# Recurrence and two-layer block on one core: rounding of the weights spread over more of the run, w_out's block sums on VectorE, loads in another order, earlier turns of the activations

## The chip, the cores and the metric

One core of a Trainium2 chip. The metric is device time in microseconds (us) of one launch, from the first to the last instruction. Timed runs of one job share their runs of the kernel before on the same chip, and every ratio below is the mean time of one kernel's fast runs over the mean of the other's fast runs in the same rounds, so it is not quite the ratio of the medians quoted.

Engines: PE is TensorE (PEld its weight loads), DVE is VectorE, ACT is ScalarE, POOL is GpSimd, SP is the queue that issues most DMAs.

## The reference

A gated linear recurrence gives x of 3072 tokens by 384 features. A two-layer block follows:

```python
f = 1.0 / (1.0 + np.exp(-f_logit))               # (4, 8, 768, 48)
for t in range(S):
    state = f[:, :, t, :, None] * state + einsum('bhd,bhe->bhde', k[:, :, t], v[:, :, t])
    y[:, :, t] = einsum('bhd,bhde->bhe', q[:, :, t], state)
x = y.transpose(0, 2, 1, 3).reshape(3072, 384)
h = x @ w_in                                     # 384 x 2048, float64 as given
g = h * erf(softplus(h))
out = g @ w_out                                  # 2048 x 384, float64 as given
```

## The kernel before

The recurrence is worked in 24 chunks of 128 tokens (stages d, t, s, y for each chunk), 12 blocks of two chunks. The hidden layer of a block is four groups, each a tile of 128x1024 (512 features by 256 tokens). From block 1 on the projection multiplies sums of blocks, seven products in place of eight, for which it needs sums of the activations (`sum_h`) and of w_out (`sum_w`). The weights come as raw 64-bit words and are rounded on the chip, one Abs on ACT and six instructions on DVE for each of 16 pieces:

```python
# round_piece(i): 96 steps in all
nc.scalar.activation(out=dst, in_=high.bitcast(FP32), func=AF.Abs);  yield
nc.vector.tensor_scalar(...);          yield      # L313
nc.vector.tensor_scalar(...);          yield      # L317
nc.vector.scalar_tensor_tensor(...);   yield      # L322
nc.vector.tensor_scalar(...);          yield      # L326
nc.vector.scalar_tensor_tensor(...);   yield      # L331
nc.vector.tensor_tensor(...)                      # L336
```

The activation of a group is a generator, moved one instruction by each `act_step`. Its buffer e has two copies (`epool`, bufs=2), so the Exp of a group can start only when the product two groups back has read its own:

```python
exp(e, h)                    # ACT, L157
term(xs[0], ...); term(xs[1], ...)      # ACT Tanh, L160
times(e, xs[0], 0); times(e, xs[1], 1)  # DVE, L165
...                          # three steps of nothing
activation(e, e, Tanh)       # ACT, L559
tensor_tensor(h, h, e, mult) # DVE, L561
```

One loop issues everything, slot by slot. In each slot PE gets one matmul of the hidden layer or projection, and the other engines' instructions are issued beside it; each engine then works through its own queue in order:

```python
for it in range(n_blocks):                # "pass" in this text
    gen, n = slots(it)                    # pass 0: 96 slots (blocks 0 and 1), pass 1: 48, pass 2: 48 + 32
    ...
    for s, _ in enumerate(gen):
        due += (1 if s < 42 else 0.6 if s < 72 else 0.3) if it == 0 else 0.42 if it == 1 else 0.6
        while due >= 1:
            weights_step(); due -= 1      # one rounding step
        ...                               # loads; a stage of the recurrence where its slot has come
        if it == 0 and s == 14:
            prepare(2, 0, CPB)            # block 2's logits: a maximum on DVE, Exp and Ln on ACT
        if it < 2:
            step = it == 1 and s % 6 == 3
        elif it == 2:
            step = s % 5 in (1, 3)
        ...
        if step: act_step()
        ...                               # sum_step(): block sums
```

The stages' PSUM tiles (d, two transposes t, y) share a pool of two buffers, `ps_at`; after a transpose ACT copies q's out (L418) and ACT, later DVE, copies k's (L420, L422).

Of the kernel before, what the change touches and what calls it, by code (L numbers as in the profile page):

```python
# [48 lines left out]
ALU = mybir.AluOpType  # L49
# [25 lines left out]
def kernel(  # L75
# [10 lines left out]
    nc = tc.nc  # L86
# [36 lines left out]
    def heads(src, b, c):  # L123
        return src[b, :, c * P : (c + 1) * P, :].rearrange("h t d -> t h d")
# [95 lines left out]
    def load_f(g):  # L220
        b, c = divmod(g, NCH)
        blk, j = divmod(g, CPB)
        if j == 0:
            lts[blk] = lpool.tile([P, CPB, d_model], FP32, name="lt", tag="lt")
        nc.sync.dma_start(
            out=lts[blk][:, j, :].rearrange("t (h d) -> t h d", d=D), in_=heads(f_logit, b, c)
        )

    def load(g, what="qkv", queue=None):
        b, c = divmod(g, NCH)  # L230
        queue = queue or nc.sync
        for src, t, n in ((q, qns[g % NQ], "q"), (k, kns[g % NQ], "k")):
            if n in what:
                queue.dma_start(out=t[:].rearrange("t (h d) -> t h d", d=D), in_=heads(src, b, c))
        if "v" in what:
            queue.dma_start(
                out=vts[g % NV][:].rearrange("t (h d) -> t h d", d=D), in_=heads(v, b, c)
            )

    def half(c):  # L240
        return slice(C * c, C * (c + 1))
# [34 lines left out]
    def home_free(i):  # L276
        return all(x in rounded for x in range(i) if HOMES[x] == HOMES[i])

    def load_piece(i):

        assert home_free(i)
        n = d_ff // n_pieces
        if i < n_pieces:
            dst = w_in_sb[:, :, bass.ts(i, n)]
        else:
            m = n_ft // n_pieces
            j = i - n_pieces
            dst = w_out_sb[:, bass.ts(j, m), :]
        raw = None if wpe == 1 else raw_home(i).bitcast(U32)
        to = dst if wpe == 1 else raw.rearrange("p (t w) -> p t w", t=dst.shape[1])  # L290
        src = w_in[:, bass.ts(i, n * wpe)] if i < n_pieces else w_out[bass.ts(j, m * P), :]
        nc.sync.dma_start(out=to, in_=src.rearrange("(t p) w -> p t w", p=P))
        raws[i] = (dst, raw)
# [75 lines left out]
    def keep_busy(n):  # L369

        for _ in range(n):
            nc.tensor.matmul(busy[-1], lhsT=tri[:], rhs=tri[:], start=True, stop=True)
# [30 lines left out]
    def stage_t(g):  # L403
        if g - 1 in late:
            late.pop(g - 1)()
        pss = []
        for src in (qd, kds[g % 2]):
            ps = ps_at.tile([P, HP, P], FP32, name="ps_t", tag="at")
            flat = src[:].rearrange("t (a r) d -> t a (r d)", r=2)
            for a in range(HP):  # L410
                nc.tensor.transpose(ps[:, a, :], flat[:, a, :], ident[:])  # L411
            pss.append(ps)
            if 0 < g < FIRST and src is qd:
                keep_busy(3)
        qAs[g] = work.tile([P, 2, HP, P], FP32, name="qA", tag="qA")
        kTs[g] = work1.tile([P, HP, P], FP32, name="kT", tag="kT")
        for r in range(2):
            nc.scalar.copy(out=qAs[g][half(r), r], in_=pss[0][half(r)])  # L418
        if g < 9:
            nc.scalar.copy(out=kTs[g][:], in_=pss[1][:])  # L420
        else:
            nc.vector.tensor_copy(out=kTs[g][:], in_=pss[1][:])  # L422
# [188 lines left out]

    sum_places = places()

    def add(out, x, y, op=ALU.add, engine=nc.vector):
        engine.tensor_tensor(out=out, in0=x, in1=y, op=op)  # L615

    def sum_w(gi):
        w = w_out_sb[:, FG * gi : FG * (gi + 1), :]
        b11, b12 = w[:, 0:2, 0:DH], w[:, 0:2, DH:]
        b21, b22 = w[:, 2:4, 0:DH], w[:, 2:4, DH:]  # L620
        t = w_sums(gi)
        add(t[:, 0], b12, b11, ALU.subtract, nc.gpsimd)
        yield
        add(t[:, 1], b22, t[:, 0], ALU.subtract, nc.gpsimd)
        yield
        add(t[:, 2], b22, b12, ALU.subtract, nc.gpsimd)
        yield
        add(t[:, 3], b21, t[:, 1], ALU.subtract, nc.gpsimd)

    def blocks(h):  # L630
        return h[:, 0:2, 0:P], h[:, 2:4, 0:P], h[:, 0:2, P:], h[:, 2:4, P:]
# [158 lines left out]
    with tc.manual_schedule():  # L790

        for t in svs:
# [2 lines left out]
        load_f(0)  # L795
        load(0, "kv", nc.scalar)
        load(0, "q")
        load_f(1)
        load(1, "qk")
        load_f(2)  # L800
        load_piece(0)
        load(1, "v")
        load(2)
        load_piece(1)
        load_piece(2)
        load_f(3)
        nc.gpsimd.memset(tri[:], 1.0)
# [1 line left out]
            out=tri[:], in_=tri[:], pattern=[[1, P]], compare_op=ALU.is_ge, fill=0.0,  # L809
# [43 lines left out]
        def weights_steps(n):  # L853
            for _ in range(n):
                weights_step()
# [5 lines left out]
        keep_busy(6)  # L861
        prepare(0, 1, 2)
        stage_t(0)
        load(3, "qk")
        load_piece(3)
        stage_d(1)
# [42 lines left out]
        due = 0.0  # L909
        for it in range(n_blocks):  # L910
            gen, n = slots(it)
            if it == 0:
                todo = [(stage_s, 2), (stage_y, 2), (stage_d, 3), (stage_t, 3), (stage_s, 3), (stage_y, 3),
                        (stage_d, 4), (stage_t, 4), (stage_d, 5), (stage_s, 4), (stage_t, 5),
                        (stage_y, 4)] + stages(2)[4:]
                at = [1, 5, 6, 12, 16, 23, 34, 42, 48, 52, 60, 74, 76, 80, 88, 94]
            else:
                todo = stages(it + 2) if it + 2 < n_blocks else []
                at = [n * x // 48 for x in (2, 6, 11, 17, 25, 29, 34, 41)] if it == 1 else [int(3 + (n - 13) / max(1, len(todo)) * i) for i in range(len(todo))]
            if ADJACENT <= it + 2 < n_blocks:  # L920

                at = ([0] if it + 2 == ADJACENT else []) + [2, 26, 42, 54, 76, 90]
                at = at[: len(todo)]
            if it + 3 < n_blocks:
                prepare_at = at[todo.index((stage_d, (it + 3) * CPB))] - 14
            at, todo = deque(at), deque(todo)
            for s, _ in enumerate(gen):
                due += (1 if s < 42 else 0.6 if s < 72 else 0.3) if it == 0 else 0.42 if it == 1 else 0.6
                while due >= 1:
                    weights_step()  # L930
                    due -= 1
                if s % 6 == 3:
                    load_more()
                if at and s == at[0]:
                    at.popleft()
                    f, g = todo.popleft()
                    f(g)
                    if f in (stage_y, stage_y_s):
                        if g + NSV < n_chunks:
                            load_sv(g + NSV)  # L940
                        load_to(g + LOOK)
                        if g == 2:
                            load(5, "v")
                            load_piece(7)
                if it == 0 and s == 14:
                    prepare(2, 0, CPB)
                if it == 0 and s == 9:
                    load_f(6)
                    load_f(7)
                if s == n // 2 and it + 4 < n_blocks:  # L950
                    for j in range(CPB):
                        load_f((it + 4) * CPB + j)
                if it + 3 < n_blocks and s == prepare_at:
                    prepare(it + 3, 0, CPB)
                if it < 2:
                    step = it == 1 and s % 6 == 3
                elif it == 2:
                    step = s % 5 in (1, 3)
                else:
                    step = s % 9 in (2, 6)  # L960
                if step:
                    act_step()
                if it == 2:
                    if s == n - 6:
                        to_sum.extend(sum_h(groups[1, gi]) for gi in range(NS))
                    sum_step()
                elif it > 2:
                    if s == n_o and it < n_blocks - 1:
                        to_sum.extend(sum_h(groups[it - 1, gi]) for gi in range(NS))
                    if it == n_blocks - 1 and s % n_o == 40 and s < 2 * n_o:  # L970
                        blk = n_blocks - 2 + s // n_o
                        to_sum.extend(sum_h(groups[blk, gi]) for gi in range(NS))
                    if s < n_o or s % 3 == 0 or it == n_blocks - 1:
                        sum_step()
                if it == n_blocks - 2 and s in (5, 40):
                    next(check)
            assert not todo
# [214 lines left out]
```

## Time and profile before

628.27 us (median of 3 runs). The slots allow to cut the span where the hidden layer's 192nd and 288th matmul record ends (ends of passes 0 and 1), where the first projection's last matmul (L670) ends (pass 2), and at a short wait of the hidden layer for an output sum near 231 us:

| stretch of before | us | what limits it |
|---|---|---|
| start and pass 0, to 105.8 | 105.8 | DVE, rounding |
| pass 1, to 135.2 | 29.4 | PE, near full |
| pass 2, to 192.7 | 57.4 | PE with holes |
| start of pass 3, to 231.6 | 39.0 | a 5.90 us hole, then PE |
| the rest, to 627.6 | 396.0 | PE, full |

The page's busy digits, the stretches by engine, PE's holes and DVE's stretched instructions are in the prediction below with their reading. A timeline's rows hold start, length, engine and line, operation, names, shapes, count, and in brackets the idle time and its releaser.

```profile
140.52 1.06 ACT L157 ACTIVATE e<-Hg 128x1024 f32<-128x1024 f32 x1 [2.00 <-DVE wT L561]
149.03 1.06 ACT L157 ACTIVATE e<-wT 128x1024 f32<-128x1024 f32 x1 [1.98 <-DVE wT L561]
```

In both rows the bracket says that ACT stands for 2 us until DVE has done a product, L561.

### The profile page before, as it was taken

Reading aid. Unit: us, or ns where it says so; the run is one execution under the profiler, and the core shown is the slowest. Engines: PE = TensorE matmul, PEld = TensorE weight load, DVE = VectorE, ACT = ScalarE, POOL = GpSimd, SP = SyncE. Lnnn points to the kernel's source line nnn. Section 1 sums busy time; section 2 is a strip of 40 time slices with the busy share of each in tenths; the row PEclk is TensorE's granted clock in tenths of the full one; section 3 lists DMA queues with packets and bytes.
Section 4 is the critical chain, followed back from the end, with each engine's and each line's share of the span. In section 5 each row is a group of like instructions: output and inputs, shape, how many; then the busy total and the mean of one; then the engine's idle time right before and its main releaser. Section 6 shows DMA issues by size and latency. Waiting matters only on the chain.

```text
span 627.6 us, 13891 instructions
## 1 busy us (share of the span) xinstructions
PE 589.5 (94%) x5777; PEld 524.7 (84%) x5777; DVE 470.2 (75%) x788; ACT 382.4 (61%) x483; POOL 38.4 (6%) x49
## 2 busy tenths in 40 slices
PE   8788699998976999999999999999999999999995
PEld 7567588887644988988998998998998989989995
DVE  4998998695589778678787876797887694756751
ACT  5725457978864457756675776765775656556200
POOL 1000011010176000000000000000000000000000
PEclk9879799999989899999999999999999999999999
DMA  9997743440321043043052052052030000000000
GB/s 200 247 241 215 216 123 63 88 78 12 63 56 26 1 78 76 1 79 75 4 102 52 2 102 51 3 102 52 3 76 14 2 27 1 19 8 1 25 26 29
DMA packets 155587, 41.35 MB, mean 66 GB/s; under 512 B 147328, under 2 KB 150400, under 8 KB 155520
## 3 DMA queue, kind: packets, MB, share of 16 engines
q1 hardware_dynamic: 153440, 40.02, 29.3%
q8 instruction: 47, 0.77, 0.5%
q10 hardware_dynamic: 2080, 0.39, 0.3%
q14 instruction: 20, 0.16, 0.1%
HBM read 35.59 MB, written 4.72 MB: 64 GB/s over the span
## 4 chain that ended last, share of the span: by engine, by line
PE 72%; DVE 12%; issue 6%; ACT 5%; DMA 2%; SPq 1%; POOL 1%; DVEq 0%; ACTq 0%; POOLq 0%
PE ops L717 31%; PE hps L587 29%; PE y L525 3%; PE ps_t L411 2%; PE ops L670 2%; PE ps_d L380 2%; DVE sv L438 1%; PE sc L460 1%; PE sc L468 1%; DVE sv L439 1%; DVE w_in_sb L322 1%; DMA qn<-in_q_dram 1%; DVE qA L496 1%; DVE w_in_sb L336 1%; ACT L160 1%
## 5 line engine op out<-in xcount | busy, mean ns | idle before, releaser
L587 PE MATMUL hps<-xT,w_in_sb 128*128 128x256 f32 x1152 | 264.7, 386 | 7.8 <-DVE w_in_sb L336 4.4
L587 PEld LDWEIGHTS hps<-xT,w_in_sb 128*128 128x128 f32 x1152 | 218.2, 192 | 41.2 <-DVE w_in_sb L336 3.4
L165 DVE SCALAR_TENSOR_TENSOR e<-x,e 128x1024 f32<-128x1024 f32 x96 | 120.2, 1252 | 13.5 <-ACT x L160 13.2
L160 ACT ACTIVATE x<-Hg,serf_bias 128x1024 f32<-128x1024 f32 x88 | 97.6, 1141 | 0.2
L157 ACT ACTIVATE e<-Hg 128x1024 f32<-128x1024 f32 x44 | 46.6, 1058 | 77.0 <-DVE Hg L561 73.2
L717 PE MATMUL ops<-wT,Hg 128*128 128x192 f32 x352 | 87.6, 331 | 0.0
L717 PE MATMUL ops<-wT,scratch 128*128 128x192 f32 x320 | 76.5, 331 | 5.9 <-DVE scratch L615 5.9
L717 PE MATMUL ops<-w_out_sb,Hg 128*128 128x192 f32 x352 | 72.6, 329 | 0.0
L561 DVE TENSOR_TENSOR Hg<-Hg,e 128x1024 f32<-128x1024 f32 x44 | 54.6, 1240 | 22.5 <-ACT e L559 22.4
L717 PEld LDWEIGHTS ops<-wT,Hg 128*128 128x128 f32 x352 | 62.1, 192 | 2.2
L594 ACT COPY Hg<-hps 128x1024 f32<-128x1024 f32 x44 | 44.4, 1010 | 31.0 <-PE hps L587 30.7
L717 PEld LDWEIGHTS ops<-w_out_sb,Hg 128*128 128x128 f32 x352 | 60.7, 192 | 2.6
L717 PEld LDWEIGHTS ops<-wT,scratch 128*128 128x128 f32 x320 | 57.0, 193 | 6.2 <-issue 6.2
L559 ACT ACTIVATE e<-e 128x1024 f32<-128x1024 f32 x48 | 50.4, 1050 | 6.4 <-DVE e L165 6.3
L496 DVE TENSOR_TENSOR qA<-sc,tri 64x256 f32<-64x256 f32 x68 | 28.7, 422 | 22.3 <-PE sc L468 21.3
L725 DVE TENSOR_TENSOR scratch<-scratch,ops 128x384 f32<-128x384 f32 (+1 forms) x44 | 22.2, 504 | 30.3 <-ACT scratch L733 25.0
L418 ACT COPY qA<-ps_t 64x512 f32<-64x512 f32 x48 | 27.7, 578 | 22.5 <-PE ps_t L411 20.6
L395 DVE TENSOR_TENSOR qd<-qn,dp 128x384 f32<-128x384 f32 x24 | 13.4, 556 | 35.6 <-ACT dp L383 34.4
L717 PE MATMUL ops<-w_out_sb,scratch 128*128 128x192 f32 x160 | 39.5, 328 | 0.0
L525 PEld LDWEIGHTS y<-qA,sv 128*32 128x32 f32 x1536 | 24.6, 113 | 17.2 <-issue 9.2
L525 PE MATMUL y<-qA,sv 128*32 128x64 f32 x1536 | 28.9, 226 | 9.3 <-issue 6.9
L438 DVE TENSOR_TENSOR sv<-sc,sv 48x192 f32<-48x192 f32 x80 | 28.4, 354 | 8.3 <-ACT qA L488 6.9
(109 smaller groups left out, 648.9 us busy)
## 6 DMA issues: line engine op xcount, KB each, us to landing
lt<-in_f_logit_dram SPq DMA_DIRECT2D x24, 192.0 KB, 3.8
qn<-in_q_dram SPq DMA_DIRECT2D x24, 192.0 KB, 3.3
out_dram<-scratch SPq DMA_DIRECT2D x12, 384.0 KB, 2.6
kn<-in_k_dram SPq DMA_DIRECT2D x23, 192.0 KB, 3.5
vt<-in_v_dram SPq DMA_DIRECT2D x23, 192.0 KB, 3.6
sv<-in_v_dram SPq DMA_DIRECT2D x84, 48.0 KB, 2.9
w_out_sb<-in_moe_w_in_dram SPq DMA_DIRECT2D x4, 768.0 KB, 6.3
Hg<-in_moe_w_in_dram SPq DMA_DIRECT2D x4, 768.0 KB, 6.4
```

Of the source, the lines that this page charges most:

```text
L157: nc.scalar.activation(out=dst[:], in_=h, func=AF.Exp)
L160: nc.scalar.activation(out=dst[:], in_=h, func=AF.Tanh, bias=serf_bias[:, i : i + 1], scale=SERF_KAB[i][0])
L165: nc.vector.scalar_tensor_tensor(out=e[:], in0=x[:], scalar=SERF_KAB[i][2], in1=e[:], op0=ALU.add, op1=ALU.mult)
L418: nc.scalar.copy(out=qAs[g][half(r), r], in_=pss[0][half(r)])
L438: nc.vector.tensor_tensor(out=new, in0=add, in1=old, op=ALU.add)
L496: nc.vector.tensor_tensor(out=qA[half(1 - r), r, :, half(c)], in0=sc[half(c), r], in1=tri1[half(c)].unsqueeze(1).broadcast_to((C, HP, C)), ...
L525: nc.tensor.matmul(y[M * i : M * (i + 1), kt, half(c)], lhsT=sv[:, r, c, a, o : o + M], rhs=qA[:, r, a, half(c)], start=(n == 0), stop=Tru ...
L559: nc.scalar.activation(out=e[:], in_=e[:], func=AF.Tanh, scale=SERF_C)
L561: nc.vector.tensor_tensor(out=h, in0=h, in1=e[:], op=ALU.mult)
L587: nc.tensor.matmul(hps[:, j, :], lhsT=w_in_sb[:, kt, ft * P : (ft + 1) * P], rhs=xTs[blk][:, kt, :], start=(kt == 0), stop=(kt == n_k - 1),)
L594: nc.scalar.copy(out=gr["h"], in_=hps[:])
L717: nc.tensor.matmul(place[n], lhsT=x[:, j, :], rhs=y, start=(gi == 0 and j == 0 and n in first), stop=(gi == n_g - 1 and j == 1), skip_grou ...
```

## The change

Its intent: round a piece when it is due and not as soon as possible, so that DVE is free for the recurrence in pass 0; take w_out's sums off GpSimd, whose instructions stretch DVE's; bring w_in's first pieces earlier; start the activations in pass 0 so that they are not late in pass 2.

```diff
-        add(t[:, 0], b12, b11, ALU.subtract, nc.gpsimd)
+        add(t[:, 0], b12, b11, ALU.subtract)            # VectorE; likewise the other three
 ...
         load(0, "q")
+        load_piece(0)
         load_f(1)
-        load(1, "qk")
+        load(1, "qkv")
+        load_piece(1)
         load_f(2)
-        load_piece(0)
-        load(1, "v")
         load(2)
-        load_piece(1)
         load_piece(2)
 ...
         stage_t(0)
+        weights_steps(2)
 ...
-                due += (1 if s < 42 else 0.6 if s < 72 else 0.3) if it == 0 else 0.42 if it == 1 else 0.6
+                due += (1 if s < 18 else 0.46 if s < 66 else 0.3) if it == 0 else 0.45
 ...
-                if it < 2:
-                    step = it == 1 and s % 6 == 3
+                if it == 0:
+                    step = s >= 24 and s % 8 == 5
+                elif it == 1:
+                    step = s % 5 == 3
```

More of the change, by code (lines that the diff above doesn't have):

```diff
@@ L612, with add @@
     sum_places = places()
-    def add(out, x, y, op=ALU.add, engine=nc.vector):
-        engine.tensor_tensor(out=out, in0=x, in1=y, op=op)
+    def add(out, x, y, op=ALU.add):
+        nc.vector.tensor_tensor(out=out, in0=x, in1=y, op=op)
     def sum_w(gi):
@@ L621, in sum_w @@
         t = w_sums(gi)
-        add(t[:, 0], b12, b11, ALU.subtract, nc.gpsimd)
+        add(t[:, 0], b12, b11, ALU.subtract)
         yield
-        add(t[:, 1], b22, t[:, 0], ALU.subtract, nc.gpsimd)
+        add(t[:, 1], b22, t[:, 0], ALU.subtract)
         yield
-        add(t[:, 2], b22, b12, ALU.subtract, nc.gpsimd)
+        add(t[:, 2], b22, b12, ALU.subtract)
         yield
-        add(t[:, 3], b21, t[:, 1], ALU.subtract, nc.gpsimd)
+        add(t[:, 3], b21, t[:, 1], ALU.subtract)
     def blocks(h):
```

## The prediction

> **What bounds the kernel now.** I read first the page's busy shares in 40 slices (15.7 us each), to see whether one limit holds for the whole span.
>
> ```profile
> PE   8788699998976999999999999999999999999995
> DVE  4998998695589778678787876797887694756751
> PEclk9879799999989899999999999999999999999999
> DMA  9997743440321043043052052052030000000000
> ```
>
> TensorE (PE) is full from slice 14 (220 us) to the end. Only the first 210 us have holes, and there VectorE (DVE) stands at 8 or 9 in slices 2 to 6. I then cut the early part at the program's own stages, told from the order of matmuls: to 28.3 us the start; 28.3 to 105.7 pass 0 (the loop's first 96 slots, one logical matmul a slot, recorded as two); to 135.2 pass 1 (48 slots); to 192.5 pass 2 (48 slots of the hidden layer, 32 of the first projection). The busy-time table by stretch, pass 0 split at 54.3 and pass 2 at 164.3 (columns: stretch, length, busy PE, PEld, DVE, ACT, POOL, granted clock, DMA share, GB/s):
>
> ```profile
> 28.28:54.30 26.02, 23.01 (x258) 18.31 (x258) 23.17 (x43) 10.88 (x19) 0.48 (x1) 0.75 0.88 208
> 54.30:105.70 51.40, 44.19 (x478) 36.66 (x478) 48.77 (x78) 25.91 (x42) 5.32 (x8) 0.93 0.61 162
> 105.70:135.20 29.50, 29.09 (x374) 24.41 (x374) 22.07 (x38) 26.84 (x39) 3.15 (x4) 1.00 0.42 73
> 135.20:164.30 29.10, 27.00 (x302) 22.14 (x300) 17.37 (x24) 23.48 (x29) 1.50 (x2) 1.00 0.29 52
> 164.30:192.50 28.20, 24.42 (x136) 15.16 (x137) 23.55 (x24) 18.96 (x24) 18.10 (x14) 0.94 0.24 43
> 192.50:203.00 10.50, 4.60 (x84) 3.77 (x82) 10.30 (x15) 5.63 (x7) 6.30 (x5) 0.95 0.16 39
> ```
>
> Pass 0 has DVE busy 71.9 of 77.4 us: it is DVE's. Passes 1 and 2 have DVE idle for 7 and 12 us. So DVE is overloaded early and idle in the middle. The last row is again DVE's: 10.30 of 10.5. The holes behind this, from PE's timeline (the bracket is the idle time before the row and its releaser):
>
> ```profile
> 28.28 2.05 PE L587 MATMUL hps<-xT,w_in_sb 128*128 128x256 f32 x4 [1.44 <-DVE w_in_sb L336]
> 45.34 1.22 PE L587 MATMUL hps<-xT,w_in_sb 128*128 128x256 f32 x2 [2.99 <-DVE w_in_sb L336]
> 72.22 1.09 PE L411 MATMUL ps_t<-ident,qd 128*128 128x128 f32 x4 [5.62 <-DVE qd L395]
> 178.22 2.05 PE L525 MATMUL y<-qA,sv 128*32 128x64 f32 x64 [3.78 <-issue]
> 203.00 0.98 PE L717 MATMUL ops<-wT,scratch 128*128 128x192 f32 x2 [5.90 <-DVE scratch L615]
> ```
>
> The first two wait for a rounded piece of w_in. The third waits for qd, a small product that stood in DVE's queue behind roundings of pieces not yet needed. The last waits for block sums of the activations while GpSimd (POOL) was computing w_out's block sums. To see what those do to DVE I compared its groups between 172 and 199 us, and after 203 us when POOL is quiet:
>
> ```profile
> L165 DVE SCALAR_TENSOR_TENSOR e<-x,e 128x1024 f32<-128x1024 f32 x6 | 10.4, 1740 | 1.0 <-ACT x L160 1.0
> L615 DVE TENSOR_TENSOR scratch<-Hg 128x256 f32<-128x256 f32 x2 | 2.4, 1220 | 0.0
> ...
> L165 DVE SCALAR_TENSOR_TENSOR e<-x,e 128x1024 f32<-128x1024 f32 x18 | 22.0, 1220 | 2.7 <-ACT x L160 2.6
> L615 DVE TENSOR_TENSOR scratch<-Hg 128x256 f32<-128x256 f32 x9 | 3.8, 419 | 0.0
> ```
>
> Beside POOL's sums an activation product takes 1.74 us in place of 1.22, a block sum 1.22 in place of 0.42.
>
> **What the Trainium skill says.** "SBUF — State Buffer", Who interferes with whom: a DVE instruction with two SBUF inputs contends with a GpSimd instruction that reads SBUF, and one blocks for the whole of the other. The trace agrees: the two-input forms grow by 0.5 to 0.8 us beside POOL's 1 to 2 us sums. "GPSIMD Engine Reference", Elementwise — side-by-side cycle accounting, has GpSimd 1.96 times as slow as DVE on a float32 tensor_tensor; here one w_out sum takes 0.99 to 1.99 us on POOL, and DVE's product of the same 128x384 size (qd) takes 0.556. "TensorE: Matmul & The Clock Gate", Why this matters for your kernels: avoid PE idle gaps over about 3 us, or the clock halves. The trace agrees: the clock is 0.50 from 30 to 38 us; after the 5.90 us gap a projection matmul starts 0.32 us after the one before it until about 208.5, then 0.16. So a closed gap is worth more than its length.
>
> **The change part by part.** One piece of raw words costs DVE two ops of 0.555, one of 0.56 and three of 0.96, so 4.55 us; the 16 pieces take 96 steps, 0.76 us each, and one 0.92 us Abs on ScalarE (ACT) a piece.
>
> (a) Rate. Before, 10 steps precede the loop, and pass 0 takes 42 + 18 + 7 = 67, pass 1 the rest. After, 12 precede it, then 18 + 22 + 9 = 49 in pass 0, 22 in pass 1, some 13 in pass 2 (over by its slot 30, before the projection at 48 needs w_out). Pass 0 loses 18 steps, 13.7 us of DVE; pass 1 gains about 2 us, pass 2 10 us. Due times hold: w_in's piece 4 is needed at slot 36 and ready at 18, piece 7 needed at 66, ready at 57.
>
> (b) Activation. Before, steps ran 0, 8, 32 in passes 0 to 2; after, 9, 10, 32. Ten steps take one group through, five start the next, so this is some 2 groups earlier: each 3.66 us of DVE (three ops of 1.22) and 4.4 us of ACT (1.06 + 2 x 1.15 + 1.05). It moves about 8 us of DVE work ahead of the first block sums. This is not saved work.
>
> (c) w_out's sums. 16 x 0.555 = 8.9 us more on DVE. Adding up the excess of each DVE op over its quiet length from 172 to 199 us gives 9.8 us of slowing, which goes. DVE's total is level or 1 us better, and POOL's 16 sums (23.4 us together in its timeline, ending at 198.9) leave the path.
>
> (d) Loads. Chunk tensors move at about 215 GB/s, pieces at 340 to 390 (from the start cut in 0.75 us slices). w_in's first piece then lands near 7.5 us in place of 12.5, and chunk 1's logits near 8.4, used at 9.03 before: no loss. Chunk 2's logits land near 14.2 against a use at 13.5, about 1 us late. The two early rounding ops fill DVE's idle time there. I expect the first hidden matmul to stay at 28 to 29 us.
>
> Replaying the queues by hand with these durations:
> Pass 0 to slot 24: piece 2 is ready near 42 in place of 45.3, so that 3 us gap closes; DVE stays full, because the first pieces are due as fast as it can make them, and slot 24 comes only 1.5 to 2 us sooner. Slots 24 to 96: PE's own work is 144 x 0.216 + 10.6 us for the attention stages, about 42; before they took 48.2 (57.5 to 105.7). DVE's is 28 steps (21.3), attention (11.4), three activation products (3.7), so 36.4, and fits. The 5.62 us gap and the slow clock after it go. Pass 0 saves 7.7 us.
> Pass 1: PE 28.4, DVE about 26, ACT about 27: length unchanged, 29 us.
> Pass 2: PE's own work is 20.7 + 20.8 + 7.6 = 49 of the 57.3 before. In its first 30 slots DVE is asked for 3.2 us in every 2.15 us of PE and falls 6 to 8 us behind; most uses stand 12 to 17 slots after their issue, which forgives about 8. ACT too is asked for about 35 us in 26, as before. I give back half of the 8 us: 3 to 4 saved.
> Pass 3's start: the 5.90 us gap and about 2.7 us of half clock after it. DVE will still be some 3 to 5 us behind, so I count 4 to 6 of these 8.6.
> Sum: 7.7 + 3.5 + 5 = 16.2, plus about 1 for a 1.07 us wait at 231 us, which has the same backlog behind it: 17. After that PE is full in both kernels and the savings simply shift the end: 628.3 - 17 = 611.
>
> A check from DVE alone: it has worked 163 us when the sum that ends the last gap is done (202.9 us). After: 163 + 8 (activations) + 8.9 - 9.8 = 170, of which 5 before 12.6 us. At 95% busy: 12.6 + 165 / 0.95 = 186, that is 17 us sooner, with the clock's 2.7 on top, if passes 0 to 2 balance nearly perfectly. They won't quite, so this is the good end, 608.
>
> **Rivals.** *DVE becomes the bound of pass 2.* For: it takes rounding, sums and activations together there. Against: it had 12 us idle in it. If the backlog lasts to the first block sums, pass 2 saves nothing and the gap at pass 3's start stays: only pass 0's 8 us are left, 619 to 620.
> *ACT becomes the bound.* Its copies free the PSUM buffers of the hidden layer, and in pass 2 they already lag by up to 8 us (a 0.77 and a 0.42 us wait of PE show it). If its Tanh also waits for a late DVE, PE stalls more: 616 to 618.
> *The start slips.* If the early piece delays chunk 1 and 2 more than I count, 2 to 3 us are lost, cancelling the early gain: 613 to 614.
> *Everything balances*: DVE's figure plus the clock, 605 to 608.
>
> **Range and chances.** 2% is 615.7 us. The central replay and the good end lie below, with the slipping start; the two engine-bound rivals lie above. No part adds work to PE or to the steady passes, so slower is nearly out. Predicted 611, range 602 to 620; faster by over 2% 0.67, within 2% 0.32, slower 0.01.
>
> **What will show it.** POOL at about 15 us busy (38.4 now, less 23.4 for the sums), and the two-input DVE ops at 1.22 and 0.42 throughout. No 5.62 us wait for qd; pass 0 ending near 98. Rounding instructions until about 145 us. The first matmul on block sums waiting under 3 us. It would be wrong if pass 2 takes 57 us again with PE waiting for DVE or ACT (then work was only moved), or if the start passes 30 us.

## The result, and the profile after

633.21 us median (633.04 to 633.91, 4 runs) against 628.72; ratio 1.0075, 95% interval 1.0049 to 1.0102. So the kernel is within 2% and a little slower, where 611 us was forecast and 602 to 620 given as the range. The profiled runs are 631.6 and 627.6 us long. The busy digits of the changed kernel, 40 slices of 15.8 us:

```profile
PE   7977999986898999999999999999999999999895
DVE  4998696899689976787877795897787783746651
POOL 1000001110000000000000000000000000000000
PEclk8877999999799899999999999999999999999999
```

Counted from 1, POOL is empty from slice 10 on, and DVE is lower in slices 5 and 7 and higher in 8, 10 and 11, as the change wants it. But PE has a 6 in slice 10 (142 to 158 us) and the clock a 7 in slice 11, where before stood 8 and 9. The same cuts as before give:

| stretch | before | after | difference | the prediction's |
|---|---|---|---|---|
| start and pass 0 | 105.8 | 104.8 | -1.0 | -7.7 |
| pass 1 | 29.4 | 32.6 | +3.2 | 0 |
| pass 2 | 57.4 | 60.9 | +3.5 | -3.5 |
| start of pass 3 | 39.0 | 35.3 | -3.7 | -6 |
| the rest | 396.0 | 398.0 | +2.0 | 0 |
| sum | 627.6 | 631.6 | +4.0 | -17 |

The first row holds the start too: the first hidden matmul comes at 30.09 us, before at 28.28, so the pass itself gained 2.8.

The engines from slot 24 to the end of pass 0, in pass 1, and in the 48 slots of the hidden layer in pass 2 (columns as in the prediction):

```profile
60.58:104.76 44.18, 43.91 (x414) 36.20 (x414) 33.28 (x55) 31.82 (x46) 3.26 (x6) 0.94 0.59 153
104.76:137.33 32.57, 29.54 (x374) 24.40 (x374) 27.36 (x42) 26.63 (x40) 4.62 (x4) 1.00 0.38 67
137.33:173.50 36.17, 29.23 (x300) 24.13 (x299) 29.87 (x41) 25.29 (x32) 1.50 (x2) 0.86 0.23 41
```

From 60.58 us on in pass 0, DVE works only 33.28 of 44.18 us: it has 11 us to spare where it was the bound. In the hidden part of pass 2 it works 29.87 of 36.17 us, against 17.37 of 29.10 in the prediction's cut of that part before. The spare time was made in one place and the work put down in another. PE's holes:

```profile
57.19 0.43 PE L525 MATMUL y<-qA,sv 128*32 128x64 f32 x4 [3.43 <-POOL qA L491]
60.58 7.70 PE L587 MATMUL hps<-xT,w_in_sb 128*128 128x256 f32 x22 [0.57 <-ACT xT L529]
72.20 0.60 PE L411 MATMUL ps_t<-ident,qd 128*128 128x128 f32 x4
...
159.49 2.05 PE L525 MATMUL y<-qA,sv 128*32 128x64 f32 x64 [6.94 <-issue]
...
206.09 1.01 PE L717 MATMUL ops<-wT,scratch 128*128 128x192 f32 x2 [3.41 <-DVE scratch L615]
```

The 5.62 us wait for qd has gone: the row at 72.20 has no bracket. It starts at the same time as before, 72.22. The holes of 1.44 and 2.99 us for w_in have gone as well. In their place there is a hole of 3.43 us at 57 us with 22 matmuls at 0.35 us each behind it (7.70 us, where the same 22 took 5.02 before), and one of 6.94 us in pass 2, again with half clock behind it (y takes 2.05 us, where the same y took 1.21 before). The hole before the block sums shrank from 5.90 to 3.41.

How the 6.94 us come about is in the timelines of ACT and DVE between 139 and 160 us. ACT first:

```profile
139.47 1.05 ACT L559 ACTIVATE e<-e 128x1024 f32<-128x1024 f32 x1
140.78 0.48 ACT L386 ACTIVATE kd<-ps_d 128x384 f32<-128x384 f32 x1
146.78 1.06 ACT L157 ACTIVATE e<-Hg 128x1024 f32<-128x1024 f32 x1 [5.51 <-DVE Hg L561]
...
157.15 1.06 ACT L157 ACTIVATE e<-wT 128x1024 f32<-128x1024 f32 x1 [3.04 <-DVE wT L561]
158.22 1.17 ACT L418 COPY qA<-ps_t 64x512 f32<-64x512 f32 x2
```

and DVE:

```profile
141.05 0.56 DVE L326 TENSOR_SCALAR Hg<-w_out_sb 128x768 uint32<-128x768 uint32 x1
141.65 0.96 DVE L331 SCALAR_TENSOR_TENSOR Hg<-Hg 128x768 f32<-128x768 uint32 x1
142.52 1.22 DVE L165 SCALAR_TENSOR_TENSOR e<-x,e 128x1024 f32<-128x1024 f32 x1
143.66 0.95 DVE L336 TENSOR_TENSOR w_out_sb<-Hg,w_out_sb 128x768 f32<-128x768 f32 x1
...
145.46 1.22 DVE L561 TENSOR_TENSOR Hg<-Hg,e 128x1024 f32<-128x1024 f32 x1
```

The Tanh that L561 needs was done at 140.5. L561 stood in DVE's queue for 5 us more, behind four rounding instructions (from 140.06), one activation product and qd and kd. Until then ACT could not start the next Exp, because that Exp writes the buffer that L561 reads, and everything behind the Exp in ACT's queue waited too: the Exp at 157.15 held the copies L418 of the ninth chunk's transposed q, which PE had made at 148. y's weight load starts at 159.46, 0.07 us after those copies end (158.22 + 1.17 = 159.39). y takes its PSUM buffer from the same pool of two. In the runs undo_act, late and pace below the same 0.07 us stand between the two, which is why I take the buffer for the link.

That DVE is no longer stretched beside POOL is plain from its groups between 172 and 199 us, the counterpart of the groups in the prediction:

```profile
L165 DVE SCALAR_TENSOR_TENSOR e<-x,e 128x1024 f32<-128x1024 f32 x7 | 8.5, 1219 | 0.0
L615 DVE TENSOR_TENSOR wT<-w_out_sb 128x384 f32<-128x384 f32 x6 | 3.3, 552 | 0.0
L615 DVE TENSOR_TENSOR scratch<-Hg 128x256 f32<-128x256 f32 x1 | 0.4, 418 | 0.0
```

### The profile page after: what moved, and what is told of

Read it like the earlier page. It is cut to its first block, busy times and chain, and to the rows that moved or that the text cites. A ratio compares the mean times of both kernels' runs of the same rounds, so it can differ in the third digit from the quotient of the medians.

```text
span 631.6 us, 13869 instructions
## 1 busy us (share of the span) xinstructions
PE 593.2 (94%) x5777; PEld 526.2 (83%) x5777; DVE 467.7 (74%) x804; ACT 383.9 (61%) x485; POOL 15.4 (2%) x33
## 4 chain that ended last, share of the span: by engine, by line
PE 68%; DVE 16%; ACT 7%; issue 3%; DMA 3%; SPq 2%; POOL 0%; ACTq 0%; DVEq 0%
PE ops L717 29%; PE hps L587 27%; PE ops L670 3%; PE y L525 3%; PE ps_t L411 2%; DVE sv L438 2%; DVE e L165 2%; DVE sv L439 2%; DVE qA L496 1%; ACT x L160 1%; PE ps_d L380 1%; PE sc L460 1%; PE sc L468 1%; DMA sv<-in_v_dram 1%; ACT L160 1%
## 5 line engine op out<-in xcount | busy, mean ns | idle before, releaser
L165 DVE SCALAR_TENSOR_TENSOR e<-x,e 128x1024 f32<-128x1024 f32 x96 | 117.5, 1224 | 15.5 <-ACT x L160 15.2
L561 DVE TENSOR_TENSOR Hg<-Hg,e 128x1024 f32<-128x1024 f32 x44 | 53.7, 1221 | 17.6 <-ACT e L559 17.4
L717 PEld LDWEIGHTS ops<-wT,scratch 128*128 128x128 f32 x320 | 56.6, 193 | 3.7 <-DVE scratch L615 3.7
L559 ACT ACTIVATE e<-e 128x1024 f32<-128x1024 f32 x48 | 50.4, 1051 | 6.6 <-DVE e L165 6.5
L525 PE MATMUL y<-qA,sv 128*32 128x64 f32 x1536 | 31.5, 230 | 17.7 <-issue 10.2
L525 PEld LDWEIGHTS y<-qA,sv 128*32 128x32 f32 x1536 | 25.9, 116 | 26.6 <-issue 18.8
L725 DVE TENSOR_TENSOR scratch<-scratch,ops 128x384 f32<-128x384 f32 (+1 forms) x44 | 22.1, 503 | 32.5 <-ACT scratch L733 27.2
L418 ACT COPY qA<-ps_t 64x512 f32<-64x512 f32 x48 | 27.7, 577 | 7.3 <-PE ps_t L411 7.0
```

Source lines behind the costliest of these rows:

```text
L165: nc.vector.scalar_tensor_tensor(out=e[:], in0=x[:], scalar=SERF_KAB[i][2], in1=e[:], op0=ALU.add, op1=ALU.mult)
L418: nc.scalar.copy(out=qAs[g][half(r), r], in_=pss[0][half(r)])
L525: nc.tensor.matmul(y[M * i : M * (i + 1), kt, half(c)], lhsT=sv[:, r, c, a, o : o + M], rhs=qA[:, r, a, half(c)], start=(n == 0), stop=Tru ...
L559: nc.scalar.activation(out=e[:], in_=e[:], func=AF.Tanh, scale=SERF_C)
L561: nc.vector.tensor_tensor(out=h, in0=h, in1=e[:], op=ALU.mult)
L717: nc.tensor.matmul(place[n], lhsT=x[:, j, :], rhs=y, start=(gi == 0 and j == 0 and n in first), stop=(gi == n_g - 1 and j == 1), skip_grou ...
```

## The experiments

Theory 1: rounding moved into pass 2 makes DVE late there, and the lateness reaches PE through ACT's queue. Theory 2: w_out's sums on DVE are what costs. Theory 3: the start slips and costs it. Each kernel's profile, cut as above. The profile is one run, and differences under 2 us in its passes 0 to 2 are not to be read alone: before and sums_only issue the same instructions through pass 0, and it took 105.8 and 107.3 us; undo_act and late do so too, with 103.0 and 103.9. One reason for this can be seen in the traces: the granted clock is either 1.00 or 0.50, each 0.50 stretch that begins between 10 and 210 us lasts 3.4, 6.8 or 10.2 us, and they don't lie at the same places in two runs of the same instructions (27.8 to 38.1 us in before, 35.5 to 42.4 in sums_only).

| run | median us | ratio to before | pass 0 | pass 1 | pass 2 | pass 3's start | rest |
|---|---|---|---|---|---|---|---|
| before | 628.7 to 629.4 | 1 | 105.8 | 29.4 | 57.4 | 39.0 | 396.0 |
| the change | 633.2 | 1.0075 | 104.8 | 32.6 | 60.9 | 35.3 | 398.0 |
| undo_sums | 639.3 | 1.0153 | 104.6 | 32.6 | 63.2 | 39.0 | 398.3 |
| undo_rate | 634.1 | 1.0069 | 112.9 | 30.7 | 54.0 | 37.0 | 398.5 |
| undo_act | 626.9 | 0.9960 | 103.0 | 30.3 | 60.4 | 34.5 | 396.0 |
| undo_start | 630.6 | 1.0011 | 104.3 | 33.4 | 58.3 | 35.3 | 398.0 |
| late | 627.1 | 0.9966 | 103.9 | 30.3 | 64.3 | 31.4 | 395.6 |
| pace | 619.6 | 0.9862 | 102.7 | 29.4 | 55.0 | 33.1 | 395.6 |
| prep2 | 630.0 | 0.9988 | 101.0 | 32.6 | 60.9 | 36.6 | 398.5 |
| sums_only | 622.4 | 0.9885 | 107.3 | 29.4 | 54.4 | 34.7 | 395.6 |
| act_only | 636.8 | 1.0124 | 109.2 | 30.3 | 59.1 | 39.0 | 397.5 |
| rate_only | 630.7 | 1.0032 | 100.3 | 29.5 | 64.5 | 37.3 | 396.3 |
| pace_prep | 615.5 | 0.9781 | 101.1 | 29.4 | 55.0 | 34.7 | 396.0 |
| pace_prep_start | 614.1 | 0.9761 | 96.1 | 29.5 | 56.6 | 34.4 | 396.0 |

All kernels gave correct results. The changed kernel was timed in its own job only, so a run is set against it through the two ratios to before or, more loosely, by the medians.

**undo_sums**: the change without the sums on VectorE.

```diff
-        add(t[:, 0], b12, b11, ALU.subtract)
+        add(t[:, 0], b12, b11, ALU.subtract, nc.gpsimd)   # and the other three
```

> The changed kernel with w_out's block sums back on GpSimd, all else kept. Theory 1 (rounding moved into the second and third pass makes VectorE late there, and ScalarE stands in its in-order queue behind VectorE): the 6.94 us hole of TensorE near 152 us stays within 1 us, and the hole before the first product on block sums grows from 3.4 back to about 6 us, so 636 us. Theory 2 (the sums on VectorE are what costs): faster, 629 us or less, and the hole near 152 us shrinks.

639.29 us, ratio 1.0153 (1.0135 to 1.0171). The hole near 152 us is again 6.94 us, and the hole before the block sums 6.25 us. Theory 2 falls: the sums on VectorE are a gain of 5 to 6 us in this kernel (4.9 by the two ratios, 6.1 by the medians), more than the 3 us that theory 1 had given them.

**undo_rate**: the change with the old rate.

```diff
-                due += (1 if s < 18 else 0.46 if s < 66 else 0.3) if it == 0 else 0.45
+                due += (1 if s < 42 else 0.6 if s < 72 else 0.3) if it == 0 else 0.42 if it == 1 else 0.6
```

> The changed kernel with the old rounding rate (a step per slot for 42 slots, then 0.6, 0.3, 0.42), all else kept. Theory 1: the 6.94 us hole near 152 us is under 2 us, the 5.6 us wait for qd in the first pass is back, and the third pass (hidden layer and first projection) gets 6 to 9 us shorter; the sum 625 to 629 us. Theory 3 (the start, 1.8 us late, and the earlier activations cost it): the time stays at 632 to 634 us.

634.12 us, ratio 1.0069 (1.0052 to 1.0086): the total missed what theory 1 expected. The places it named behave much as it said: the hole near 152 us is 1.16 us, pass 2 is 6.9 us shorter (60.9 to 54.0), and the wait for qd is back, with 3.09 us and not 5.6. But pass 0 is 8.1 us longer; PE waits there another 2.48 us for ACT's logits. So the new rate is worth 8 us in pass 0 and costs 7 in pass 2 and 2 in pass 1.

**undo_act**: the change with the old activation turns.

```diff
-                if it == 0:
-                    step = s >= 24 and s % 8 == 5
-                elif it == 1:
-                    step = s % 5 == 3
+                if it < 2:
+                    step = it == 1 and s % 6 == 3
```

> The changed kernel with the old activation turns (none in the first pass, 8 steps in the second), all else kept. Theory 1: VectorE has 8 us less to do before the third pass, so the hole near 152 us shrinks to 0 to 3 us, but the activations are then late for the block sums, whose hole grows from 3.4 to 6 us or more; 629 to 633 us. Theory 2: no change of the hole before the sums.

626.85 us, ratio 0.9960 (0.9940 to 0.9980), better than expected, but not for the reason given: the hole near 154 us is still 5.74 us. The gain is 1.8 us in pass 0, 2.3 in pass 1, 2.0 in the rest, and under 1 in pass 2 and at the start of pass 3. And the hole before the sums, for which the early turns were made, became smaller without them: 2.71 us against 3.41. Nothing had been waiting for activations there.

**undo_start**: the change with the old loads and without the two early steps.

```diff
         load(0, "q")
-        load_piece(0)
         load_f(1)
-        load(1, "qkv")
-        load_piece(1)
+        load(1, "qk")
         load_f(2)
+        load_piece(0)
+        load(1, "v")
         load(2)
+        load_piece(1)
 ...
         stage_t(0)
-        weights_steps(2)
```

> The changed kernel with the old order of loads and without the two early rounding steps, all else kept. Theory 3 (the start slips because chunk 1's and chunk 2's logits come behind w_in's pieces): the first hidden matmul comes at 28.3 us in place of 30.1, and the kernel ends 2 us sooner or more, 631 us or less. Theory 1: the start gains 2 us but the hole near 152 us stays above 5 us; 630 to 632 us.

630.55 us (627.77 to 632.76), ratio 1.0011 (0.9974 to 1.0047). The first hidden matmul comes at 28.05 us in place of 30.09; the hole in pass 2 is 4.04 us, where theory 1 had it above 5. Theory 3's figures came true as well (28.3 us, 631 or less). The start does slip by 2 us, but the hole is still there without the slip, so the start is not the whole loss. What it costs, this run doesn't give cleanly: without the two early steps the new rate makes a piece of w_in late, and PE waits for it, at half clock after the wait, as it doesn't in the changed kernel:

```profile
83.13 6.95 PE L587 MATMUL hps<-xT,w_in_sb 128*128 128x256 f32 x18 [3.15 <-DVE w_in_sb L336]
```

**late**: undo_act with the rest of the rounding held back inside pass 2.

```diff
-                due += (1 if s < 18 else 0.46 if s < 66 else 0.3) if it == 0 else 0.45
+                due += (1 if s < 18 else 0.46 if s < 66 else 0.3) if it == 0 else 0 if it == 2 and s < 29 else 0.45
```

> The run undo_act with one edit: the some 13 rounding steps left for the third pass are held back until its slot 29, behind the issue of the eighth chunk's y; they are due by slot 60 or so. Theory 1 (those steps make VectorE late with the activation product, ScalarE's next Exp waits for it and the copies behind the Exp hold TensorE's y): the 5.74 us hole before y near 154 us is under 2 us, and the kernel ends 4 to 6 us before undo_act, at 621 to 623 us. Rival (the hole comes from the number of activations in the pass, not from the rounding): the hole stays over 4 us and the time within 1 us of 627.

627.12 us, ratio 0.9966 (0.9949 to 0.9983). PE's holes in pass 2 of this run:

```profile
151.36 1.22 PE L525 MATMUL y<-qA,sv 128*32 128x64 f32 x64 [1.99 <-issue]
165.33 4.14 PE L670 MATMUL ops<-w_out_sb,wT 128*128 128x384 f32 x12 [1.50 <-ACT Hg L594]
178.19 2.05 PE L525 MATMUL y<-qA,sv 128*32 128x64 f32 x64 [2.69 <-issue]
191.32 7.12 PE L670 MATMUL ops<-w_out_sb,wT 128*128 128x384 f32 x16 [3.73 <-DVE wT L561]
```

The hole before y went from 5.74 to 1.99 us as theory 1 said: the rounding makes it. But the time didn't move. The same DVE work 30 slots later opened 1.50, 2.69 and 3.73 us elsewhere, the last a projection matmul that waits for the product L561 itself. So the fault is not the place of one instruction: at neither of the two places tried did pass 2 have room for the rounding.

**pace**: undo_act with the rest of the rounding done in pass 0's idle time.

```diff
-                due += (1 if s < 18 else 0.46 if s < 66 else 0.3) if it == 0 else 0.45
+                due += (1 if s < 18 else 0.46 if s < 30 else 0.62) if it == 0 else 0.45
```

> The run undo_act with the first pass's rate at 1 a slot up to slot 18, 0.46 up to slot 30, then 0.62, so that no rounding is left for the third pass. VectorE would be busy some 45 of the 45 us from slot 24 on in the first pass. Theory 1: the hole before y near 154 us falls under 2 us; the first pass gets 2 to 4 us longer; 622 to 626 us. If the first pass can't take it, the qd wait is back and the time is 627 to 630 us.

619.57 us (617.64 to 622.11), ratio 0.9862 (0.9833 to 0.9890), 2.4 us below what was expected. Pass 0 is 102.7 us, no longer than without the extra steps (103.0): DVE did have the room. The hole before y is 1.51 us and pass 2 5.4 us shorter than in undo_act, pass 1 0.9; pass 2's 55.0 us are close to the 54.4 of sums_only, which moves no rounding. With late this settles theory 1.

**prep2**: the change with block 2's logits prepared earlier.

```diff
-                if it == 0 and s == 14:
+                if it == 0 and s == 2:
                     prepare(2, 0, CPB)
```

> The changed kernel with the preparation of block 2's logits issued at slot 2 of the first pass in place of slot 14. Theory: the 3.43 us hole before y near 57 us (and the half clock after it, some 2.5 us) comes from ScalarE waiting for VectorE's maximum on these logits with the score copies behind it. Then that hole falls under 1.5 us and the first pass ends 3 to 5 us sooner; the hole near 152 us takes part of it back; 629 to 631 us. Rival (VectorE itself is late there): the hole stays.

629.95 us (625.27 to 631.44), ratio 0.9988 (0.9949 to 1.0028). The hole near 57 us:

```profile
55.85 0.30 PE L525 MATMUL y<-qA,sv 128*32 128x64 f32 x4 [1.59 <-issue]
```

1.59 us in place of 3.43 (just above the 1.5 named), and pass 0 ends 3.8 us sooner. The same kind of link as in pass 2, with another waiter: ACT's Exp of the logits waited for a DVE maximum at the end of a queue of roundings (ACT's wait before it was 3.51 us), and the score copies stood behind it. The hole in pass 2 stayed at 6.94 us, and of 3 us the times show about 3, within a wide spread.

**sums_only**: the kernel before with only the sums on VectorE.

```diff
-        add(t[:, 0], b12, b11, ALU.subtract, nc.gpsimd)
+        add(t[:, 0], b12, b11, ALU.subtract)               # and the other three
```

> The kernel before with only w_out's sums moved to VectorE. Theory: the slowing beside GpSimd (9.8 us of VectorE time) is gone and 8.9 us of sums come in, so VectorE's load is level, but y at 178 us and the block sums are no longer behind stretched instructions: the 3.78 and 5.90 us holes fall to about 1.5 and 3 us, the end 4 to 6 us sooner: 623 to 626 us. Rival (the holes come from lateness alone): within 1 us of the kernel before.

622.42 us, ratio 0.9885 (0.9864 to 0.9907), better than expected. The two holes that stood beside POOL's sums:

```profile
177.44 1.21 PE L525 MATMUL y<-qA,sv 128*32 128x64 f32 x64 [1.51 <-issue]
...
198.29 0.59 PE L717 MATMUL ops<-wT,scratch 128*128 128x192 f32 x2 [2.71 <-DVE scratch L615]
```

3.78 became 1.51 and 5.90 became 2.71, and both matmul rows run at full clock (1.21 and 0.59 us, where before they took 2.05 and 0.98). Pass 2 and the start of pass 3 take 7.3 us less. DVE's own load was level, so the gain is in the order of things: no stretched instruction in front of one that PE waits for.

**act_only**: the kernel before with only the new turns.

```diff
-                if it < 2:
-                    step = it == 1 and s % 6 == 3
+                if it == 0:
+                    step = s >= 24 and s % 8 == 5
+                elif it == 1:
+                    step = s % 5 == 3
```

> The kernel before with only the new activation turns. Theory A (early turns put activations in front of ScalarE's copies in the second pass and shift their phase against the later passes, and nothing waited for them): the second pass gets 1 to 3 us longer, the part after the first store's wait near 230 us takes 398 us in place of 396 (as in all five runs with the early turns so far), and the time is 630 to 634 us. Rival B (the turns only cost beside the rounding moved into the third pass): 626 to 629 us.

636.83 us, ratio 1.0124 (1.0108 to 1.0141), worse than theory A's range. Passes 0, 1 and 2 are 3.4, 0.9 and 1.7 us longer, the rest 1.5. The hole before the sums is 5.89 us, as in before (5.90): the early turns bring nothing at the place for which they were made. Rival B falls: they cost without the moved rounding too. The 3.4 us of pass 0 come in at one place:

```profile
95.12 1.63 PE L380 MATMUL ps_d<-lt,tri 128*128 128x384 f32 x2 [2.24 <-ACT lt L365]
```

The clock is 0.50 from 95.2 to 98.6 us. ACT had stood there for 5.87 us until DVE had done the maximum of these logits (L360), at 92.76 us, before at 91.05: two activation products now stood ahead of it in the queue of DVE, busy 36.8 of the 38 us from 57 to 95. ACT's added table load, at 86.19, lies in front of that wait and cost nothing here. Since sums_only, with the old turns, has a wait of 2.04 us at the same place and a pass 0 longer by 1.5 than before, not all of the 3.4 need be the turns'.

The wait near the end that all six runs with the new turns have (1.66 to 1.68 us), and none of the others, is this one of the changed kernel, PE and then DVE:

```profile
592.25 0.56 PE L717 MATMUL ops<-wT,qn 128*128 128x192 f32 x2 [1.68 <-DVE scratch L725]
```

```profile
587.97 1.22 DVE L561 TENSOR_TENSOR Hg<-Hg,e 128x1024 f32<-128x1024 f32 x1
589.11 1.22 DVE L165 SCALAR_TENSOR_TENSOR e<-x,e 128x1024 f32<-128x1024 f32 x1
590.24 0.42 DVE L615 TENSOR_TENSOR Hg<-Hg 128x256 f32<-128x256 f32 x1
590.58 1.52 DVE L725 TENSOR_TENSOR scratch<-scratch,ops 128x384 f32<-128x384 f32 x3
```

L725 empties the PSUM buffers of the projection. In the run undo_act its three stand before the activation products in this part of DVE's queue (L725 at 581.82, the next products from 583.26), and PE doesn't wait. Nine turns more in pass 0 and one in pass 1 shift which activation instruction falls in which slot for the whole run, and in the last pass they happen to fall in front of the sums. All six runs with the new turns have 397.5 us or more in the last stretch, all others 396.3 or less.

**rate_only**: the kernel before with only the new rate.

```diff
-                due += (1 if s < 42 else 0.6 if s < 72 else 0.3) if it == 0 else 0.42 if it == 1 else 0.6
+                due += (1 if s < 18 else 0.46 if s < 66 else 0.3) if it == 0 else 0.45
```

> The kernel before with only the change's rounding rate. Theory 1: the 5.6 us wait for qd goes, but the third pass gets the rest of the rounding and a hole of 4 to 6 us with half clock before y near 152 us; GpSimd's sums stay; 627 to 632 us, so no gain. Rival (the rate is the part that gains, as the prediction had it): 619 to 623 us.

630.67 us, ratio 1.0032 (1.0015 to 1.0049), as theory 1 had it. Pass 0 is 5.5 us shorter, where the prediction hoped for 7.7; a wait of 2.01 us for a piece of w_in at 81.90, as in undo_start, is in it. Pass 2 is 7.1 us longer, with a 5.33 us hole before y.

**pace_prep**: pace with `prepare(2, ...)` at slot 2, as in prep2.

```diff
-                if it == 0 and s == 14:
+                if it == 0 and s == 2:
                     prepare(2, 0, CPB)
```

> The run pace with block 2's logits prepared at slot 2: the 4.08 us hole before y near 57 us falls under 2 us and the half clock after it goes; the first pass ends 2.5 to 4 us sooner, and since pace leaves no hole that gives it back, the kernel ends 2.5 to 4 us sooner than pace: 615.5 to 617.5 us.

615.46 us, ratio 0.9781 (0.9764 to 0.9797). The hole near 57 us is 1.59 us. Against pace it is 4.1 us by the medians.

**pace_prep_start**: pace_prep with the loads and the first steps of before (the whole edit is the one shown for undo_start).

```diff
         stage_t(0)
-        weights_steps(2)
```

> The same with the old order of loads and without the two early rounding steps: the first hidden matmul at 28 us in place of 29.5, the end 0.5 to 2 us sooner than pace_prep if the later start is what the new order costs; 0 to 1 us later than pace_prep if the two early steps pay for it.

614.12 us (613.80 to 614.45), ratio 0.9761 (0.9745 to 0.9777). The first hidden matmul comes at 27.52 us in place of 29.28. It beats both kernels: 2.4% under before, 3.0% under the change by the medians. Of the change it keeps the sums on VectorE and the idea of a rate, and drops the early turns, the load order and the rounding in pass 2.

## Why the prediction was wrong

**The range.** 633.2 us lies outside 602 to 620, and the sign was wrong.

**(a) Rate: half right.** The gain in pass 0 was there, 5.5 us alone (rate_only) and 8.1 in the change (undo_rate) against 7.7 forecast, and the wait for qd went. The step that failed is in pass 2: "falls 6 to 8 us behind; most uses stand 12 to 17 slots after their issue, which forgives about 8". The lateness itself was not far off: the product L561 stood 4.9 us in the queue. But I measured it against the distance of PE's uses of DVE's results alone. It reached PE by another way, DVE's product to ACT's Exp (a buffer of two) to the copies behind the Exp to a PSUM buffer of two, and ACT had no slack: by my own count it was "asked for about 35 us in 26". The rival "If its Tanh also waits for a late DVE, PE stalls more" had the right engines and named the wrong instruction. Pass 2 was to be 3.5 us shorter and was 3.5 longer. The run late shows that, without this way, the same work is paid elsewhere in the pass, so what failed is also a sum: 10 us of rounding, put where 12 us of idle time were counted. In the kernel before, every wait of DVE in pass 2 that the profile lists is for ACT (the longest 5.87 us, for the Tanh L559), and at both places where that time was filled ACT waited in turn. The last rounding ended at 172 us and not at about 145. Pass 1, forecast as unchanged, took 3.2 us more: PE waited there 0.89 us for ACT's xT, 0.92 for DVE's qd and 1.29 before y. Alone the rate adds 0.1 us to it and the turns 0.9, so this comes of both together.

**(b) Activation turns: wrong.** I took it that early turns move 8 us of DVE work ahead, harmless at worst ("This is not saved work"). Measured alone they cost 7.7 us by the medians (636.83 - 629.11), the largest loss of the four parts. The step that failed is that work moved ahead is free: in pass 0 DVE had no room in the old rate, and two products ahead of the logits' maximum reached PE through ACT (3.4 us there, act_only). Some 2 us are the shifted phase in the last pass, which I had set to nothing: "PE is full in both kernels and the savings simply shift the end". I had also counted no activation table load, and there are two more (20 against 18). The Trainium skill, "ScalarE: Activation LUTs", What ACT_TABLE_LOAD costs, has 1283 ns for the load in such a switch; the trace has 1283 ns. That these loads cost time is not shown; the one looked at, in act_only, did not. The prediction's "9, 10, 32" steps are 9, 9, 32 by the code. How the rest divides is not separated by these runs.

**(c) w_out's sums: right, and under-sized in its consequence.** POOL has 15.4 us, 15 were forecast; the products take 1.219 us and the sums 0.418 us. Alone it gives 1.15% or about 7 us; the prediction had no separate gain for it.

**(d) Loads: the rival was right.** Chunk 1's logits were used at 9.58 us after a wait of DVE for the DMA, 8.4 was forecast; chunk 2's at 15.81, 14.2 forecast. After PE's hole of 1.96 us before 11.1 us its clock was 0.50 from 11.4 to 21.7 (0.83 in the mean of the start, 0.99 before), and the first hidden matmul came at 30.09 us, not 28 to 29; the eight runs with the new start have it at 29.3 to 30.1, the six with the old at 27.5 to 28.3. The rival "The start slips" said 2 to 3 us; undo_start gives 2.7, less its own late piece.

**Pass 0's slot 24** was to come 1.5 to 2 us sooner; with y it came 3.1 us later (60.58 against 57.49), because block 2's logits waited in DVE's queue and ACT's score copies behind them (prep2). The same error as in pass 2: only direct uses were followed.

**What would show it**: both signs of being wrong came true. "If pass 2 takes 57 us again with PE waiting for DVE or ACT": it took 60.9. "If the start passes 30 us": 30.09, though only just. Of the signs of being right POOL's 15.4 us and the missing wait for qd came; pass 0 ended at 104.8 and not near 98, and the first matmul on block sums waited 3.41 us and not under 3.

**A reading of the clock.** The prediction has the trace agree with the skill's idle gaps over 3 us because "the clock is 0.50 from 30 to 38 us". That stretch (27.8 to 38.1) stands beside gaps of 1.19 and 1.44 us, so it is no case of that rule.

The parts nearly add: sums -1.15%, turns +1.24%, rate +0.32%, each alone, and the start +0.64% (the change's 1.0075 less undo_start's 1.0011), together +1.05% against +0.75% measured. The intervals are 0.2 to 0.5% each way, and the parts act on each other: the rate costs 0.32% alone, but 0.06% in the change (1.0075 less 1.0069).

## What to carry to other kernels

When work is moved to an engine's idle time, ask first what that idle time was: if the engine was waiting for a neighbour that in turn waits for it through a buffer of two, there may be no room there, however low its busy share; here there was none. Follow a late instruction through every in-order queue that waits for it, and not only to its direct user; the instructions behind the waiter are late too. And measure the parts of such a change alone: one of four was worth 1.15%, one cost 1.24%, and going back on the turns and the loads, with the rounding put into the stretch where the engine was really free and one block's logits prepared earlier, turned a loss of 0.75% into a gain of 2.4%.

## What the Trainium skill lacked or had wrong

- "ScalarE: Activation LUTs", What ACT_TABLE_LOAD costs: the page adds a drain of about 1380 ns to each load, about 2.66 us in total. Here the load takes 1.283 us and the next activation starts 1.29 us after the load began (load at 165.82, 0.02 us after the end of the activation before it, Tanh at 167.11 in the changed kernel); no drain of that size is seen.
- "SBUF — State Buffer", Who interferes with whom: that a two-input DVE instruction contends with a GpSimd instruction that reads SBUF agrees. Besides two ratios for the two orders of issue, the page has no size for a stream of both: here a DVE product of 1.22 us took 1.74 us in the mean and 2.03 at most, and removing the neighbour was worth 1.15% of the kernel though 8.9 us of sums came onto DVE.
- "TensorE: Matmul & The Clock Gate", Why this matters for your kernels: it asks for no idle gaps over about 3 us. In the start of the changed kernel matmuls ran at half clock after one gap of 1.96 us before 11.1 us, the only one over 0.4 us since the first matmul (0.50 granted from 11.4 us on), so 3 us was not a safe bound here. All five runs with a gap of 1.91 to 1.97 us there lost the clock by 12.8 us, the three with 1.21 to 1.28 us didn't; a gap of 1.76 us at 18.57 us in the kernel before did no harm (1.00 until 27.8).
- No page that I found treats a wait that travels through a third engine's in-order queue; here one DVE product 5 us late became ACT waits of 5.51 and 3.04 us and a PE hole of 6.94 us.
